# Two gated feed-forward layers behind a chunked attention on one core: operand tiles at fixed places, operand work at four points of a pass, gate-value products behind the sums

## The chip, the cores and the metric

The kernel runs on one core of a Trainium2 chip, as one program. Its metric is device time in microseconds (us): the median of three runs was 1138.36 us (1136.27 to 1138.62). One further execution was taken with the profiler: 1139.58 us, of which 1137.8 us is the span from the first to the last instruction. All rows below come from that one.

## The reference, cut to what matters

```
attention: B=4, H=8, S=768, D=64; chunks of 32 queries, each over 8 memory keys and a window
           (16 to the left, the chunk, 8 to the right); softmax; out -> x [3072 tokens, 512]
moe 1:     gate = 1 / (1 + exp(-(x @ w_gate)))      w_gate, w_val [512, 1536]
           x = (gate * (x @ w_val)) @ w_out         w_out [1536, 512]
moe 2:     h = x @ w_in                             w_in [512, 2048]
           out = (h * (1 / (1 + exp(-h)))) @ w_out  w_out [2048, 512]
```

Weights arrive as 64-bit floats, seen in the kernel as pairs of 32-bit integers.

## The kernel before, in words

Every matrix product is made of three TensorE products of fp32r values: a value is split into a high part (a cast on ScalarE, ACT in the rows) and a low part (value minus high part, on VectorE, DVE). A matmul here is 128x128 by 128x512 unless said otherwise.

A weight tile is loaded as integers (a `stg` tile), scaled on ACT (`rebias`, L126) and joined to fp32 on DVE (`join`, L136 and L139). In this text a *join* is those two DVE instructions.

**Stage 1, blocks 0 to 3.** Tokens go through layer 1 in blocks of 512. For each of 12 slices `f` of the hidden width TensorE (PE) makes `pg` (12 matmuls), `pv` (12), and the output product `y` of the slice before (12 at L104 to L108). ACT makes the sigmoid (L371) and the high part of the gated value (L378); DVE makes gate times value (L376) and the low part (L381). Between these, `steps(0)`, `steps(1)` and `steps(2)` are called after `pg`, after `pv` and after the output product. They carry the attention of the later tiles (`events`: *meet* is scores and the tile before's output, then *exp*, *norm* and *turn*, the transposes to `pt` with the copy to `at`). In block 0 they carry also the layer 1 weights (`Feed.step`), in blocks 1 to 3 the operand work of later stages (`prep.go`). At the end of a block the next block's `x` is split (L96 on ACT, L99 on DVE).

**Stage 2, block -1.** The last 1024 tokens go through layer 1 by a seven-product scheme for 2x2 blocks of the matrices: 12 *passes*, gate (`-1_0g`) and value (`-1_0v`) in turn, then the output product `out2` with 252 matmuls. **Stage 3** takes layer 2 in three blocks (`0_0` to `0_7` are the passes of the first one), each with its `out2` of 336 matmuls.

A pass (`pair2`, L985) makes seven products of six matmuls each, in the order A11, S1, S2, A12, S3, S4, A22, in three PSUM banks: c1 takes A11 and A12, c3 takes S1 and S4, c2 takes S2, S3 and A22. Between two products in one bank the first one has to be read: `s1` (copy of c1, ACT, L1032), `s5` (copy of c3, ACT, L1036, to which GpSimd, POOL, adds s1), the *u sum* (c2 + s1 on DVE, before S3 may start), the *s5 sum* (c2 + s5 on DVE, before A22 may start), then u again from c3 and s1 from c2. Every second pass (odd `p`, not a gate pass) leaves a *tail* to the pass behind it: a difference of two 128x1024 tiles (L973) and the split of one tile for the output product (`gf`, L96 on ACT, L99 on DVE), issued right after the copy `s1`.

**Operand work.** Stages 2 and 3 need the weights in the form of the seven operands, split in high and low. `Pair2` makes them for a pair of layer 2 tiles: two rebias, two joins, four sums of 128x256 (L633), then four tiles `coi` or `coo` (the last one half as long), each with a high cast on ACT (L754) and a low part on DVE (L641), and a store to DRAM. `PairC` does the like for layer 1 (`ccg`, `ccv`, `cco`). `Pace` meters this work: `go(us)` is called at a step of stage 1, or after every second product in a pass (L1012), and runs pieces as long as the given budget lasts; `later` holds a store back for `LAG` calls of `go`, `co` hands out the operand tiles from one pool of 7 buffers (6 in stage 2 and 3) that the loads use too. The pool's next buffer may be written when what used it last is done; for an operand tile that is its store.

Instructions stand on each engine in the order in which the code issues them (`manual_schedule`), so an instruction that waits holds up everything behind it on its engine. All loads and stores go through the queue of SyncE (SP). Weights for a pass come in *granules* (`next_granule`, L954) into five slots.

## Time and profile before

| | |
|---|---|
| median of 3 runs | 1138.36 us |
| profiled execution, own time | 1139.58 us |
| its span | 1137.8 us |
| PE busy | 1097.2 us (96%), 7580 instructions |
| DVE busy | 772.7 us (68%) |
| ACT busy | 534.9 us (47%) |
| POOL busy | 66.7 us (6%) |
| chain of waits that ended last | PE 84%, DMA 8%, DVE 5%, ACT 1%, SP's queue 1% |

PE is busy nearly throughout, so what counts is where it is not, or where it is slow. The busy time of a matmul in the rows has a modelled end, so the distance between the starts of two matmuls is safer than their length. A wait is put down to the engine whose instruction ended last before it; what that instruction itself waited for is read one row further.

### The profile page before, as it was taken

What the parts mean: (1) busy time and instruction counts of PE and PEld (TensorE: products, weight loads), DVE (VectorE), ACT (ScalarE), POOL (GpSimd) and SP (SyncE); (2) the same over time, 40 slices, a digit from 0 to 9 for tenths busy, and PEclk for the clock granted to TensorE, in tenths of its full rate; (3) what the DMA queues carried; (4) which work ended last, traced back from release to release, by engine and by line L of the source; (5) the groups of instructions that cost most, each with busy time, mean ns of one, the idle gap of its engine ahead of it and who ended that gap; (6) DMA issues with size and microseconds to landing.
All of it is one profiled execution on the core that took longest, in us unless ns stands there. A gap on an engine that the chain in (4) does not pass through costs nothing.

```text
span 1137.8 us, 18863 instructions
## 1 busy us (share of the span) xinstructions
PE 1097.2 (96%) x7580; PEld 893.0 (78%) x7580; DVE 772.7 (68%) x1156; ACT 534.9 (47%) x791; POOL 66.7 (6%) x50
## 2 busy tenths in 40 slices
PE   7999999979999999998989997999999999999998
PEld 4888888868777888776777885888888888888887
DVE  7988876667677687566767975458843479543665
ACT  6767554534435453343435544444534455344442
POOL 0000000000000000011110101101011110011000
PEclk9999999989999999999999999999999999999999
DMA  8788678768779897589879586875665666655552
GB/s 330 249 286 296 257 254 298 264 241 286 272 237 319 274 332 282 211 281 323 293 244 384 185 265 240 299 294 186 232 213 194 223 248 226 226 195 204 188 215 78
DMA packets 106247, 288.02 MB, mean 253 GB/s; under 512 B 8624, under 2 KB 39344, under 8 KB 95408
## 3 DMA queue, kind: packets, MB, share of 16 engines
q1 hardware_dynamic: 105872, 286.43, 71.9%
q8 instruction: 60, 0.98, 0.4%
q10 hardware_dynamic: 288, 0.39, 0.1%
q14 instruction: 27, 0.22, 0.1%
HBM read 210.24 MB, written 76.55 MB: 252 GB/s over the span
## 4 chain that ended last, share of the span: by engine, by line
PE 84%; DMA 8%; DVE 5%; ACT 1%; SPq 1%; issue 0%; ACTq 0%; DVEq 0%
PE o L1141 20%; PE c L1005 19%; PE pg L361 11%; PE pv L361 10%; DMA w2o_d<-coo 5%; PE y L104 3%; PE y L106 3%; PE y L108 3%; PE sx L310 1%; PE sx L222 1%; PE o_-1_1_6471 L1141 1%; PE o_-1_0_6470 L1141 1%; PE pt L294 1%; PE c_-1_3g L1005 1%; PE c_-1_1g L1005 1%; PE c_-1_0v L1005 1%
## 5 line engine op out<-in xcount | busy, mean ns | idle before, releaser
L1005 PE MATMUL c<-xp,wr 128*128 128x512 f32 x1008 | 231.7, 391 | 7.1 <-DVE u L970 3.3
L1141 PE MATMUL o<-gf,wr 128*128 128x512 f32 x1008 | 229.0, 389 | 0.0
L1005 PEld LDWEIGHTS c<-xp,wr 128*128 128x128 f32 x1008 | 189.9, 189 | 48.4 <-DVE u L970 3.7
L1141 PEld LDWEIGHTS o<-gf,wr 128*128 128x128 f32 x1008 | 189.2, 188 | 39.3
L361 PE MATMUL pg<-x,w 128*128 128x512 f32 x564 | 138.2, 394 | 6.3 <-ACT x L96 6.2
L361 PE MATMUL pv<-x,w 128*128 128x512 f32 x564 | 139.0, 395 | 2.1 <-DVE sg L376 2.0
L99 DVE TENSOR_TENSOR gf<-g,gf 128x1024 fp32r<-128x1024 f32 x84 | 103.9, 1240 | 50.5 <-ACT gf L96 50.0
L361 PEld LDWEIGHTS pg<-x,w 128*128 128x128 f32 x564 | 106.7, 190 | 29.7 <-ACT x L96 6.7
L96 ACT CAST gf<-g 128x1024 fp32r<-128x1024 f32 x84 | 88.1, 1052 | 86.8 <-PE o L1141 71.4
L361 PEld LDWEIGHTS pv<-x,w 128*128 128x128 f32 x564 | 103.9, 188 | 26.3 <-DVE sg L376 3.0
L970 DVE TENSOR_TENSOR s<-c,s 128x512 f32<-128x512 f32 x48 | 33.2, 691 | 58.4 <-PE c L1005 58.4
L378 ACT CAST g<-sg 128x512 fp32r<-128x512 f32 x48 | 29.7, 620 | 75.3 <-DVE sg L376 75.2
L973 DVE TENSOR_TENSOR g<-g,g 128x1024 f32<-128x1024 f32 x48 | 58.4, 1216 | 0.0
L381 DVE TENSOR_TENSOR g<-sg,g 128x512 fp32r<-128x512 f32 x48 | 33.1, 690 | 35.6 <-ACT g L378 35.6
L976 ACT ACTIVATE g<-s 128x512 f32<-128x512 f32 x48 | 30.3, 632 | 56.2 <-DVE s L970 56.2
L1037 POOL TENSOR_TENSOR s<-s,s 128x512 f32<-128x512 f32 x24 | 35.9, 1497 | 328.9 <-ACT s L1036 280.7
L970 DVE TENSOR_TENSOR u<-c,s 128x512 f32<-128x512 f32 x24 | 16.5, 689 | 49.1 <-PE c L1005 49.1
L371 ACT ACTIVATE sg<-pg 128x512 f32<-128x512 f32 x48 | 28.6, 597 | 28.8 <-PE pg L361 28.6
L271 ACT ACT_TABLE_LOAD x21 | 26.9, 1283 | 30.0 <-DVE e L263 28.1
L104 PE MATMUL y<-g,wor 128*128 128x512 f32 x144 | 40.0, 400 | 0.0
L106 PE MATMUL y<-g,wor 128*128 128x512 f32 x144 | 38.7, 390 | 0.0
L108 PE MATMUL y<-g,wor 128*128 128x512 f32 x144 | 38.6, 390 | 0.0
(596 smaller groups left out, 1565.3 us busy)
## 6 DMA issues: line engine op xcount, KB each, us to landing
wr<-w2o_d SPq DMA_DIRECT2D x42, 1024.0 KB, 4.8
wr<-w2i_d SPq DMA_DIRECT2D x24, 1024.0 KB, 5.3
wor<-wo_d SPq DMA_DIRECT2D x36, 512.0 KB, 6.3
wr<-w2i_d SPq DMA_DIRECT2D x24, 768.0 KB, 4.6
w2o_d<-coo SPq DMA_DIRECT2D x56, 256.0 KB, 6.3
w2i_d<-coi SPq DMA_DIRECT2D x24, 512.0 KB, 7.2
wr<-wc_d SPq DMA_DIRECT2D x12, 1024.0 KB, 6.7
v<-in_vh_dram SPq DMA_DIRECT2D x21, 512.0 KB, 5.5
```

The costliest lines, as they stand in the source:

```text
L96: nc.scalar.copy(hi, src)
L99: lo_eng.tensor_tensor(out=lo, in0=src, in1=hi.bitcast(F32), op=ALU.subtract)
L104: nc.tensor.matmul(o, w_hi, x_hi, start=first, stop=False)
L106: nc.tensor.matmul(o, w_hi, x_lo, start=False, stop=False)
L108: nc.tensor.matmul(o, w_lo, x_hi, start=False, stop=last)
L361: nc.tensor.matmul(o[:, :n], w[:, pw, kt * P : (kt + 1) * P], x[kt][:, px, :n], start=i == 0, stop=i == len(steps) - 1,)
L381: nc.vector.tensor_tensor(out=g[:, 1, :n], in0=sg[:, :n], in1=g[:, 0, :n].bitcast(F32), op=ALU.subtract)
L970: nc.vector.tensor_tensor(out=o, in0=a, in1=b_, op=ALU.add)
L973: nc.vector.tensor_tensor(out=o, in0=a, in1=b_, op=ALU.subtract)
L1005: nc.tensor.matmul(o, w[:, pw, m, kt * P : (kt + 1) * P], X[i][:, px, kt], start=first and j == 0, stop=j == 5, skip_group_check=not first,)
L1037: nc.gpsimd.tensor_tensor(out=s5, in0=s5, in1=s1, op=ALU.add)
L1141: nc.tensor.matmul(c[at[i], dp], w[:, pw, pl, dp * P : (dp + 1) * P], f[:, px, pl], start=i in (A11, S1, S2) and pp == 0 and j == 0, stop= ...
```

## The change

Operand tiles get tags of their own, `co0` to `co3` and, in stage 1, `stg2` and `stg3`, used in turn; loads of `Pair2` go to `stg0` and `stg1`. A tag is taken again only when its store was issued at least three calls of `go` before (`REST`); until then the operand work stands still. Stores are held back for 2 calls instead of 4. In block 0 the loads of layer 1 weights turn over 4 buffers instead of 7; the pool of sigmoid tiles has 4 buffers instead of 5. In a pass `go` is called at four points, with a budget by kind of pass and point, none in the first gate pass. In a value pass the gate-value products (L1026 before, L1057 now) stand behind the DVE sums. In stage 1, for tiles from 8 on, *exp*, *norm* and *turn* come one step later.

```diff
-PREP2 = 0.9
+PREP2 = {"g": (0.4, 0.6, 1.1, 1.1), "v": (0.7, 0.7, 0.3, 0.3), "l": (0.9, 0.9, 1.1, 1.1)}
...
-            self.pool, self.bufs = None, 7
+            self.pool, self.tag = None, None
...
-                [P, 512, 2], I32, tag="stg", name=f"stg_{self.name}", bufs=self.bufs
-            )
+            self.stg = pool.tile([P, 512, 2], I32, tag=self.tag, name=f"stg_{self.name}")
...
-        sg = hold[0].tile([P, 512], F32, tag="sg", name=f"sg{name}", bufs=5)
+        sg = hold[0].tile([P, 512], F32, tag="sg", name=f"sg{name}", bufs=4)
...
+        for n, u in enumerate(units):
+            u.tag = f"stg{n % 4}"
...
-                    events.setdefault(at + 1, []).append(("exp", t))
-                events.setdefault(at + (2 if fast else 4), []).append(("norm", t))
-                events.setdefault(at + (4 if fast else 6), []).append(("turn", t))
+                    events.setdefault(at + 2, []).append(("exp", t))
+                events.setdefault(at + (3 if fast else 4), []).append(("norm", t))
+                events.setdefault(at + (5 if fast else 6), []).append(("turn", t))
...
-                high(0)
-                high(1)
-                yield None
-                for c in range(4):
-                    lo_of(cos[c], f32s[:, 2 * c : 2 * c + cos[c].shape[2]])
-                    pace.later(lambda c=c, co=cos[c]: self.store(c, co))
-                    if c + 2 < 4:
-                        high(c + 2)
-                    yield 0.7 if c < 3 else 0.4
+                for c in range(6):
+                    if c < 4:
+                        while pace.busy():
+                            yield None
+                        high(c)
+                    if c == 1:
+                        yield None
+                    if c >= 2:
+                        c -= 2
+                        lo_of(cos[c], f32s[:, 2 * c : 2 * c + cos[c].shape[2]])
+                        pace.later(lambda c=c, co=cos[c]: self.store(c, co))
+                        yield 0.7 if c < 3 else 0.4
...
-            LAG = 4
+            LAG, REST = 2, 3
...
+            def busy(self):
+                at = self.free[self.tag(self.n)]
+                return at is None or at + self.REST > self.step
...
-                while len(self.fifo) >= self.cap:
-                    self.fifo.pop(0)[1]()
-                return co_tile(pool, name, self.bufs)
+                tag = self.tag(self.n)
+                assert self.free[tag] is not None
+                self.n += 1
+                self.free[tag] = None
+                return co_tile(pool, name, tag)
...
-                if b < 0 or b == 0 and p < NPAIR - 2:
-                    beats[0] += 1
-                    if beats[0] % 2 == 0:
-                        prep.go(PREP2)
...
                 elif kind == "v":
-                    nc.vector.tensor_tensor(out=g, in0=c, in1=g, op=ALU.mult)
+                    wait.append((g, c))
...
+            def mult():
+                while wait:
+                    g, c = wait.pop(0)
+                    nc.vector.tensor_tensor(out=g, in0=c, in1=g, op=ALU.mult)
+
+            def beat(n):
+                if b < 0 or b == 0 and p < NPAIR - 2:
+                    prep.go(PREP2[kind if kind else "l"][n] if p or kind == "v" or b == 0 else 0.0)
...
             prod(c1, A11, True)
             nc.scalar.copy(s1, c1)
             if tail:
                 tail()
+            beat(0)
             prod(c3, S1, True)
             nc.scalar.copy(s5, c3)
             nc.gpsimd.tensor_tensor(out=s5, in0=s5, in1=s1, op=ALU.add)
             if fill:
                 fill()
+            beat(1)
             prod(c2, S2, True)
             add(u2, c2, s1)
             prod(c1, A12, False)
             done("11", c1)
             prod(c2, S3, False)
             add(s5, c2, s5)
+            mult()
             done("22", s5)
+            beat(2)
             prod(c3, S4, False)
             add(u2, c3, u2)
+            mult()
             done("12", u2)
             prod(c2, A22, False)
             add(s1, c2, s1)
             done("21", s1)
+            mult()
+            beat(3)
...
-                prep = Pace(items, 7, 4)
+                prep = Pace(items, ["stg2", "stg3", "co0", "co1", "co2", "co3"])
...
-        prep = Pace([Pair2("o", p, pool) for p in range(NPAIR)], 6, 3)
+        prep = Pace([Pair2("o", p, pool) for p in range(NPAIR)], ["co0", "co1", "co2", "co3"])
```

ACT at the end of block 1, from the sigmoid of the last slice to the split of the next `x`, before:

```order
L371 ACTIVATE sg_11_2913<-pg_11_2900 128x512
L271 ACT_TABLE_LOAD
L271 ACTIVATE e_2950<-e_2950 128x512
L691 CAST cco_0_3006<-fco_2895 128x512
L691 CAST cco_1_3007<-fco_2895 128x512
L96 CAST x_0_3010<-x_2_1835 128x512
```

and now:

```order
L369 ACTIVATE sg_11_2915<-pg_11_2902 128x512
L702 CAST ccv_0_3012<-fcv_2866 128x512
L702 CAST ccv_1_3014<-fcv_2866 128x512
L96 CAST x_0_3016<-x_2_1835 128x512
L96 CAST x_1_3019<-x_2_1835 128x512
L96 CAST x_2_3022<-x_2_1835 128x512
```

The exponential (`e`) is gone from here to the next step, and the two operand casts are of another pair.

DVE from value pass `-1_1v` into gate pass `-1_2g` (`s` stands for the sums called s5 and s1, `u` for the u sum, `g` for gate-value products, the 128x1024 rows are the tail), before, from the s5 sum to the u sum:

```order
L970 TENSOR_TENSOR s_-1_1v<-c_-1_1v,s_-1_1v 128x512
L1026 TENSOR_TENSOR g-1_0_22_5531<-s_-1_1v,g-1_0_22_5531 128x512
L970 TENSOR_TENSOR u_-1_1v<-c_-1_1v,u_-1_1v 128x512
L1026 TENSOR_TENSOR g-1_0_12_5548<-u_-1_1v,g-1_0_12_5548 128x512
L641 TENSOR_TENSOR coo_3_5772<-fo_5657,coo_3_5772 128x256
L970 TENSOR_TENSOR s_-1_1v<-c_-1_1v,s_-1_1v 128x512
L1026 TENSOR_TENSOR g-1_0_21_5559<-s_-1_1v,g-1_0_21_5559 128x512
L973 TENSOR_TENSOR g-1_0_12_5548<-g-1_0_12_5548,g-1_0_11_5522 128x1024
L99 TENSOR_TENSOR gf-1_0_5812<-g-1_0_11_5522,gf-1_0_5812 128x1024
L136 TENSOR_SCALAR stg_w2o_5704<-stg_w2o_5704 128x512
L139 SCALAR_TENSOR_TENSOR fo_5821<-stg_w2o_5704 128x2x256
L970 TENSOR_TENSOR u_-1_2g<-c_-1_2g,s_-1_2g 128x512
```

and now, from the first of two joins (the s5 sum and the product `g..11` stand right ahead of it):

```order
L134 TENSOR_SCALAR stg_w2o_5633<-stg_w2o_5633 128x512
L137 SCALAR_TENSOR_TENSOR fo_5752<-stg_w2o_5633 128x2x256
L998 TENSOR_TENSOR u_-1_1v<-c_-1_1v,u_-1_1v 128x512
L1057 TENSOR_TENSOR g-1_0_22_5524<-s_-1_1v,g-1_0_22_5524 128x512
L998 TENSOR_TENSOR s_-1_1v<-c_-1_1v,s_-1_1v 128x512
L1057 TENSOR_TENSOR g-1_0_12_5533<-u_-1_1v,g-1_0_12_5533 128x512
L1057 TENSOR_TENSOR g-1_0_21_5544<-s_-1_1v,g-1_0_21_5544 128x512
L1001 TENSOR_TENSOR g-1_0_12_5533<-g-1_0_12_5533,g-1_0_11_5515 128x1024
L99 TENSOR_TENSOR gf-1_0_5788<-g-1_0_11_5515,gf-1_0_5788 128x1024
L134 TENSOR_SCALAR stg_w2o_5635<-stg_w2o_5635 128x512
L137 SCALAR_TENSOR_TENSOR fo_5752<-stg_w2o_5635 128x2x256
L998 TENSOR_TENSOR u_-1_2g<-c_-1_2g,s_-1_2g 128x512
```

The low part of an operand (`coo_3`) has left the value pass, one join has come in; the tail and a join still stand ahead of the u sum of the gate pass.

DVE from the tail to the u sum of pass `0_2` in layer 2, before:

```order
L973 TENSOR_TENSOR g_0_12_6948<-g_0_12_6948,g_0_11_6914 128x1024
L99 TENSOR_TENSOR gf_0_7053<-g_0_11_6914,gf_0_7053 128x1024
L136 TENSOR_SCALAR stg_w2o_6943<-stg_w2o_6943 128x512
L139 SCALAR_TENSOR_TENSOR fo_7062<-stg_w2o_6943 128x2x256
L970 TENSOR_TENSOR u_0_2_7044<-c_0_2_7040,s_0_2_7042 128x512
```

and now:

```order
L1001 TENSOR_TENSOR g_0_12_6892<-g_0_12_6892,g_0_11_6865 128x1024
L99 TENSOR_TENSOR gf_0_7009<-g_0_11_6865,gf_0_7009 128x1024
L641 TENSOR_TENSOR coo_0_6991<-fo_6927,coo_0_6991 128x512
L641 TENSOR_TENSOR coo_1_6993<-fo_6927,coo_1_6993 128x512
L641 TENSOR_TENSOR coo_2_7012<-fo_6927,coo_2_7012 128x512
L641 TENSOR_TENSOR coo_3_7015<-fo_6927,coo_3_7015 128x256
L998 TENSOR_TENSOR u_0_2_7000<-c_0_2_6996,s_0_2_6998 128x512
```

Where a join stood, four low parts stand.

## Rows read from the trace of the kernel before

**Rows 1.** Chain that ended last, merged, stages 2 and 3: start us, us, what.
```profile
472.08 2.72 PE c_-1_0g L1005 x12
...
667.13 6.82 PE c L1005 x30
...
753.02 76.16 PE o L1141 x336
```

**Rows 2.** Waits of PE: line waited for, total us, times, longest.
```profile
PE c_-1_2g L1005 <- DVE u_-1_2g L970: 3.4, 1, 3.4
...
PE c_-1_4g L1005 <- DVE u_-1_4g L970: 3.1, 1, 3.1
...
PE pv L361 <- DVE sg L376: 2.0, 3, 1.2
...
PE c_-1_5v L1005 <- DVE s_-1_5v L970: 1.2, 1, 1.2
...
PE o_-1_0_6466 L1141 <- DVE gf-1_2_6460 L99: 1.0, 1, 1.0
...
PE c_-1_0v L1005 <- DVE s_-1_0v L970: 0.5, 1, 0.5
```

**Rows 3.** Timeline of PE: start us, us, instruction, [idle before, releaser].
```profile
248.72 4.67 PE L361 MATMUL pg<-x,w 128*128 128x512 f32 x12 [6.23 <-ACT x L96]
...
483.58 2.25 PE L1005 MATMUL c_-1_0g<-xp-1_6_5433,wr 128*128 128x512 f32 x6 [1.98 <-ACT s_-1_0g L1036]
...
488.15 1.55 PE L1005 MATMUL c_-1_0v<-xp-1_0_5222,wr 128*128 128x512 f32 x6
...
687.15 5.73 PE L1005 MATMUL c<-xp,wr 128*128 128x512 f32 x24 [2.33 <-DVE s L970]
...
699.34 5.96 PE L1005 MATMUL c<-xp,wr 128*128 128x512 f32 x18 [3.27 <-DVE u L970]
```

**Rows 4.** PE by windows of 1 us: us, PE busy (matmuls), granted clock, DMA, GB/s.
```profile
250.00:251.00 1.00, 1.00 (x3) 0.50 1.07 395
...
688.00:689.00 1.00, 1.00 (x6) 1.00 1.01 400
```

**Rows 5.** Timeline of ACT, end of block 1 and pass -1_1v.
```profile
247.53 0.62 ACT L691 CAST cco<-fco 128x512 fp32r<-128x512 f32 x1 [5.21 <-DMA w2i_d<-coi]
...
519.97 0.41 ACT L754 CAST coo<-fo 128x256 fp32r<-128x256 f32 x1 [5.38 <-DMA w2o_d<-coo]
...
521.89 1.05 ACT L96 CAST gf-1_0_5812<-g-1_0_11_5522 128x1024 fp32r<-128x1024 f32 x1
```

**Rows 6.** Timeline of DVE in stage 2, passes -1_0v and -1_2g.
```profile
494.43 1.89 DVE L641 TENSOR_TENSOR coo<-fo,coo 128x512 fp32r<-128x512 f32 x3
...
522.08 1.22 DVE L973 TENSOR_TENSOR g-1_0_12_5548<-g-1_0_12_5548,g-1_0_11_5522 128x1024 f32<-128x1024 f32 x1
523.22 1.22 DVE L99 TENSOR_TENSOR gf-1_0_5812<-g-1_0_11_5522,gf-1_0_5812 128x1024 fp32r<-128x1024 f32 x1
524.35 1.49 DVE L136 TENSOR_SCALAR stg_w2o<-stg_w2o 128x512 int32<-128x512 int32 x1
525.88 0.69 DVE L139 SCALAR_TENSOR_TENSOR fo<-stg_w2o 128x512 int32<-128x512 int32 x1
...
527.08 0.42 DVE L136 TENSOR_SCALAR stg_w2o<-stg_w2o 128x512 int32<-128x512 int32 x1
...
529.60 1.54 DVE L633 TENSOR_TENSOR fo<-fo 128x256 f32<-128x256 f32 x4
```

**Rows 7.** Timeline of POOL, passes -1_1g and -1_2g.
```profile
502.10 1.29 POOL L1037 TENSOR_TENSOR s_-1_1g<-s_-1_1g 128x512 f32<-128x512 f32 x1 [9.03 <-ACT s_-1_1g L1036]
...
523.49 2.07 POOL L1037 TENSOR_TENSOR s_-1_2g<-s_-1_2g 128x512 f32<-128x512 f32 x1 [10.63 <-ACT s_-1_2g L1036]
```

**Rows 8.** Tile coo, its stores: time from issue to landing.
```profile
DMA to landing us min/median/max: 5.2/6.3/8.6
```

**Rows 9.** Line L121, loads into stg tiles: time from issue to landing.
```profile
DMA to landing us min/median/max: 3.4/6.5/10.4
```

More of the change, by code (lines that the diff above doesn't have):

```diff
@@ L532, in pro @@
                     pts[i // 2] = ps_att(f"pt{i}")
-                at = hold[0].tile([P, 512], F32, tag="sg", name=f"at{i}", bufs=5)
+                at = hold[0].tile([P, 512], F32, tag="sg", name=f"at{i}", bufs=4)
                 att_turn(i, pts[i // 2][:, i % 2], at)
@@ L633, in sums_of, with co_tile @@
                 nc.vector.tensor_tensor(out=at[o], in0=at[a], in1=at[b], op=op)
-        def co_tile(pool, name, bufs):
-            co = pool.tile([P, 512, 2], I32, tag="stg", name=name, bufs=bufs)
+        def co_tile(pool, name, tag):
+            co = pool.tile([P, 512, 2], I32, tag=tag, name=name)
             co = co.rearrange("p a b -> p (a b)").rearrange("p (h m k) -> p h m k", h=2, m=2)
@@ L660, in store, with stores @@
                     nc.sync.dma_start(out=out, in_=part)
+            def stores(self, ids, co):
+                if self.k == "o":
+                    for n, i in enumerate(ids):
+                        self.store(i, co[:, :, n])
+                else:
+                    self.store(ids[0], co)
             def whole(self, o, w):
@@ L694, in steps @@
                     lo_of(cos[c], f32s[:, 2 + 2 * c : 4 + 2 * c])
-                    if self.k == "o":
-                        for n, i in enumerate(ids):
-                            pace.later(lambda i=i, co=cos[c][:, :, n]: self.store(i, co))
-                    else:
-                        pace.later(lambda i=ids[0], co=cos[c]: self.store(i, co))
+                    pace.later(lambda ids=ids, co=cos[c]: self.stores(ids, co))
                     yield 0.7
@@ L710, in load @@
             def load(self, pace):
-                for u in self.units:
-                    u.pool, u.bufs = self.pool, pace.bufs
+                for j, u in enumerate(self.units):
+                    u.pool, u.tag = self.pool, f"stg{j}"
                     u.load()
@@ L755, in high, with __init__ @@
                     cos.append(co)
-                high(0)
-                high(1)
-                yield None
-                for c in range(4):
-                    lo_of(cos[c], f32s[:, 2 * c : 2 * c + cos[c].shape[2]])
-                    pace.later(lambda c=c, co=cos[c]: self.store(c, co))
-                    if c + 2 < 4:
-                        high(c + 2)
-                    yield 0.7 if c < 3 else 0.4
+                for c in range(6):
+                    if c < 4:
+                        while pace.busy():
+                            yield None
+                        high(c)
+                    if c == 1:
+                        yield None
+                    if c >= 2:
[3 more added lines that the diff above has]
+                        yield 0.7 if c < 3 else 0.4
         class Pace:
-            LAG = 4
-            def __init__(self, items, bufs, cap):
-                self.due, self.step, self.fifo, self.bufs, self.cap = 0.0, 0, [], bufs, cap
+            LAG, REST = 2, 3
+            def __init__(self, items, tags):
+                self.due, self.step, self.fifo, self.tags = 0.0, 0, [], tags
+                self.free, self.n = {t: -9 for t in tags}, 0
                 self.items, self.urgent, self.gen = list(items), [], None
@@ L777, in __init__, with tag, put @@
                 twos[0].load(self)
-            def co(self, pool, name):
-                while len(self.fifo) >= self.cap:
-                    self.fifo.pop(0)[1]()
-                return co_tile(pool, name, self.bufs)
+            def tag(self, n):
+                return self.tags[n % len(self.tags)]
+            def busy(self):
+                at = self.free[self.tag(self.n)]
+                return at is None or at + self.REST > self.step
+            def co(self, pool, name):
+                tag = self.tag(self.n)
[3 more added lines that the diff above has]
+                return co_tile(pool, name, tag)
             def later(self, store):
                 self.fifo.append((self.step, store))
+            def put(self):
+                self.fifo.pop(0)[1]()
+                tag = next(self.tag(n) for n in range(self.n, self.n + 9) if self.free[self.tag(n)] is None)
+                self.free[tag] = self.step
             def advance(self):
@@ L801, in go @@
                 while self.fifo and self.fifo[0][0] <= self.step - self.LAG:
-                    self.fifo.pop(0)[1]()
+                    self.put()
                 self.due = min(self.due + us, 2.5)
@@ L816, in finish @@
                 while self.advance() is not False:
-                    pass
+                    if self.busy():
+                        self.step += self.REST
+                        while self.fifo:
+                            self.put()
                 while self.fifo:
-                    self.fifo.pop(0)[1]()
+                    self.put()
         g_t, wo_u, yacc = {}, {}, {}
@@ L831, in sg_slot @@
         def sg_slot(name):
-            return hold[0].tile([P, 512], F32, tag="sg", name=name, bufs=5)
+            return hold[0].tile([P, 512], F32, tag="sg", name=name, bufs=4)
         def emit_out1(bi, f, tile_of=sg_slot):
@@ L1062, in pair2 @@
             return tail_of
-        gf, beats = {}, [0]
+        gf = {}
         def npp_of(b):
```

8 lines of the change are left out of this document (5 added, 3 removed).

## The prediction

> **What bounds the kernel now.** I read the chain of waits first. In stages 2 and 3 it is matmuls almost alone, so the time is the number of matmuls times their duration plus what PE loses between them. A 128x512 matmul takes 76.16 / 336 = 0.2267 us [rows 1]; a product of six 1.36, a pass of 42 9.52. The starts of the stages in the chain then give the losses. Stage 2 lasts 667.13 - 472.08 = 195.05 us for 12 passes, the output product of stage 1's last slice (12 matmuls) and 252 of `out2`, 768 in all, or 174.1: 20.95 lost. The first eight passes of stage 3 last 753.02 - 667.13 = 85.89 for 76.17: 9.7 lost. The `out2` that follows from 753.02 on is at full speed, and behind it I look for nothing [rows 1].
>
> The waits of PE name what the losses are: the u sum of the gate passes `-1_2g` and `-1_4g` (3.4 and 3.1), the s5 sum of the six value passes (0.5 the first, 1.2 the last), three waits for the gated value in stage 1 (2.0 together) and 1.0 at the start of `out2` [rows 2]. The timeline of PE adds the largest, 6.23 before 12 matmuls at the end of block 1, 1.98 in `-1_0g`, and in stage 3 2.33 and 3.27 [rows 3].
>
> A gap costs more than its length when the clock falls. The 12 matmuls behind the 6.23 took 4.67 and not 2.72; the 18 behind the 3.27 took 5.96 and not 4.08: 1.95 and 1.9 more. The 24 behind 2.33 took 5.73, 0.29 above 5.44; the 12 behind 1.98, up to the next pass at 488.15, took 4.57 and not 2.72 [rows 3]. The granted clock was 0.50 (1.2 GHz) in the first of these stretches and 1.00 (2.4 GHz) in the one behind 2.33 [rows 4]. So gaps of 3.3 and 6.2 were followed by a slow stretch, one of 2.33 was not, and one of 1.98 was: from about 2 to 3 it is open.
>
> Then what the waited-for engines themselves wait for. ACT's operand cast `cco` stood 5.21 for a store of another operand tile, with the split of the next `x` queued behind it; `coo` stood 5.38 in `-1_1v`, with the `gf` cast behind it [rows 5]. These are DMA landings (5.2 to 8.6 us after issue [rows 8]) that reach PE by way of an ACT queue. On DVE three low parts (1.89 for three) stand ahead of the s5 sum in the first value pass, and the tail (two of 1.22) and a join (1.49 and 0.69) ahead of the u sum of `-1_2g` [rows 6].
>
> **The change, part by part.**
>
> *Fixed places with REST.* An operand tile's high cast now comes at least three calls of `go` after its store was issued. In stages 2 and 3 a call comes every quarter of a pass (2.4 us) and in stage 1 every output step; together with the held store and the turn of the tags I count four to five steps, 11 us or more, from store to reuse, against landings up to 8.6 [rows 8]. So ACT's waits for stores should go. In stage 1 the 6.23 of idle falls to about 0.6 (the split itself and its way to PE), with the 1.95 of slow clock: 7.6. The three waits for the gated value (2.0) come from ACT held up in the same way, and go. Against it, block 0: a load now waits for the join four units back instead of seven, so some have 5.5 to 7 us to land, while landing takes 3.4 to 10.4, median 6.5 [rows 9]. PE and DVE have slack in block 0; I put it at 0.5 (bounds 0 and the rival below). Four sigmoid buffers can hold a sigmoid up by a store of y, at a block's start, behind work that covers it: nothing, and if that cover is gone up to the three waits' 2.0. Stage 1: **9.1**.
>
> *`-1_0g`.* There is no operand work in it now, so no rebias in front of its s5 copy. Its 1.98 of wait and the 1.85 behind it (4.57 - 2.72) go: **3.8**.
>
> *Value passes.* The lows ahead of the s5 sum and the gate-value products are gone; products come behind sums. The s5 sum can start when its product ends, as DVE has no other work then. The residue of stage 2's 20.95, after 3.8 for `-1_0g`, 5.3 for `-1_2g` and 5.0 for `-1_4g` (waits of 3.4 and 3.1 [rows 2] with 1.9 of clock each) and 1.0 for `out2`, is 5.8: the six waits of 0.5 to 1.2, with a restart behind each. Gain **5.8**. If I am wrong, and the join put into the value pass lies before a sum, 0.3 a pass come back.
>
> *`-1_2g`.* Here is what stays. Count from the pass's start, when A22 of the pass before ends. S3 may start at 5.44 (four products), if the u sum has read c2. DVE, spaced as in [rows 6] (0.6 for a 512-wide operation, 1.14 for a 1024-wide one): the s5 sum begins at -2.72, and behind it product, join, u sum, product, s1 sum and two products end at 2.8; the tail at 5.05. The second join's first part costs 0.42 alone, but 1.49 beside POOL's add [rows 6]; that add took 2.07 then and 1.29 elsewhere [rows 7]. In this pass it should run from about 3.9, so the join's first part ends at 5.95, its second at 6.6 and the u sum at 7.3: a gap of 1.9. Without the meeting of the two the u sum would end at 6.8, 0.5 earlier.
>
> *`-1_4g`.* By the same walk, with two lows and the tail ahead of the u sum and no join: 1.4.
>
> *`out2`.* The last sums no longer have products ahead of them, so its first `gf` is ready: 1.0 gained.
>
> Stage 2 would lose 1.9 + 1.4 = 3.3 before any clock price, where it lost 20.95: **17.65**.
>
> *Stage 3, first block.* `0_1`: two rebias on ACT, two joins and four sums (1.54 [rows 6]) ahead of the u sum: 1.0. `0_2`: ACT casts two operand tiles ahead of the s1 copy, so the `gf` cast (1.05 [rows 5]) ends late; then DVE's half of it, four lows (about 2.2 by 1.89 for three [rows 6]) and the u sum, ending at 8.0: 2.6. `0_4`: tail and two joins, the second beside POOL's add: 8.2, so 2.8 (1.9 without it). Together 6.4 where 9.7 were lost: **3.3**. Bounds: nothing is lost (9.7), or the walks are 1 us worse in each (0.3).
>
> *The clock.* Three gaps of 1.9 to 2.8 remain (`-1_2g`, `0_2`, `0_4`), in the open region. If all are followed by a slow stretch they cost 3 x 1.95 = 5.9, if none 0. The nearest rows stand on both sides (2.0 yes, 2.33 no), so I take half, 2.9, and 0.5 for restarts: **-3.4**.
>
> Beside POOL: both operations that met its add in the rows grew, 1.49 for 0.42 and 2.07 for 1.29 [rows 6, 7], while the 1024-wide sum with two inputs in SBUF that ran into the same add kept its 1.22 [rows 6]. The Trainium skill, GPSIMD Engine Reference, section 1 "Specifications", says that GpSimd shares its SBUF interfaces with VectorE and contends with instructions in a 2-port mode or with two SBUF inputs. For the join the trace agrees; for the two-input sum, read by its own length, it does not. By the rule, the sums and lows that I moved next to POOL's add (in `0_1` and `0_2`) would make that add, and the s5 sum behind it, later still; by the rows only the joins do, which the walks of `-1_2g` and `0_4` hold.
>
> **Sum.** 9.1 + 17.65 + 3.3 - 3.4 = 26.65. The profiled execution of 1139.58 would be 1112.9. It lies 1.22 above the median of the runs, 1138.36, so the median becomes 1111.7: **1112**.
>
> **Rivals.**
>
> *A, the stalls that I leave go too.* DVE in `-1_2g` and `0_4` is ahead of my walk, the joins miss POOL's add (0.5 and 0.9 less) and no gap brings the slow clock (2.9 less). For: a 2.33 gap left the clock at 1.00 [rows 3, 4]; the walks chain spacings that were read where DVE was loaded. Against: tail and join together are fixed work of 4 us and more. All gaps halved (3.3 + 6.4 to 4.9) and no clock price: 26.65 + 4.8 + 2.9 = 34, or about 1104.
>
> *B, the DMA waits move and don't go.* A store held back two calls still lies in SP's queue behind loads, and six tiles per pair in six buffers came round to the same place before too; what REST counts is calls, and in stage 1 calls that come close together leave less time than landings of 8.6 [rows 8]. Then operand casts still wait on ACT, with the x split and `gf` behind them. For: the 5.21 and 5.38 are of this kind [rows 5]. Against: the distances counted above. Half of stage 1's gain (4.5) and stage 3's (3.3) go, and all three gaps bring the slow clock (3.0): 1112 + 10.8, about 1123. If the tail passes moreover keep their old losses (10.3 instead of 3.3), 1130.
>
> *C, slower.* Block 0 becomes bound by loads. With four buffers each load is issued only when the join four units back is done; if the queue of SP takes each to the upper landing, 10.4, where a unit's turn leaves 7 [rows 9], a slice of block 0 waits about 3 us, and over 11 slices that is 33, more than the 26.65 gained. It decides above 26.65 / 11 = 2.4 a slice. Then 1138 + 6, about 1145. For: loads of 6.5 in the median leave little. Against: only some loads are that short of time, and the weights for a slice are wanted later than their joins.
>
> *D, nothing changes:* that would need the same loss on PE at other places; the order shows the work gone from the two largest, so little chance.
>
> **How the numbers follow.** My case 0.58, A 0.14, B 0.20, C 0.05, D 0.03. What this kernel's measurement can tell from no change is about 0.2%, 2.3 us. The likeliest case alone spans 1106 (no price for the clock, 2.9; nothing for block 0, 0.5; walks half a us too long at five places, 2.5) to 1119 (all three clock drops, 3.0; walks 1 us too short at four places). Range with most of A and B: 1102 to 1125. Faster: my case, A and nearly all of B, 0.92; same 0.03; slower 0.05.
>
> **What to look for afterwards.** Right, if ACT shows no operand cast that waited for a store for some us; if the gap at the end of block 1 is under 1 us; if value passes take 9.5 and `-1_0g` 12.2; and if PE's waits are now at `-1_2g`, `-1_4g`, `0_1`, `0_2` and `0_4`, on the u sum. Wrong, if one of these gaps is above 3; if ACT's `DMA` waits in block 1 or pass `0_2` still reach 3 us; or if block 0 ends later than before by more than a few us, with loads as what DVE or ACT waited for.

## The result, and the profile after

The changed kernel takes 1123.47 us (median of four runs, 1122.33 to 1124.43) against 1138.49 for the kernel before: a ratio of 0.9871 (95% interval 0.9853 to 0.9888). The profiled execution took 1124.10, 15.5 less than that of before, with a span of 1122.1. So it is faster, by 1.3%, and inside the range, but 15 us were gained where 27 were forecast.

What PE waits for after the change, longest in total first (total us, times, longest):

```profile
PE c L1033 <- DVE u L998: 8.4, 3, 3.5
PE sx L308 <- ACT at L293: 2.5, 2, 2.3
PE c_-1_2g L1033 <- DVE u_-1_2g L998: 2.5, 1, 2.5
PE c_-1_4g L1033 <- DVE u_-1_4g L998: 2.4, 1, 2.4
...
PE c_-1_4v L1033 <- DVE u_-1_4v L998: 0.9, 1, 0.9
PE c_-1_0v L1033 <- DVE u_-1_0v L998: 0.8, 1, 0.8
```

Against [rows 2]: the waits for s5 sums are gone, the wait for the gated value too, and what is left is on u sums; three of these, 8.4 together, are in stage 3 (the first line). The timeline of PE, at the end of block 1, early in block 3, and in stage 3:

```profile
241.66 2.88 PE L359 MATMUL pg<-x,w 128*128 128x512 f32 x12
...
367.73 0.86 PE L308 MATMUL sx<-v,at 64*32 64x64 f32 x64 [2.33 <-ACT at L293]
...
662.98 11.41 PE L1033 MATMUL c<-xp,wr 128*128 128x512 f32 x42 [2.03 <-DVE u L998]
677.93 22.14 PE L1033 MATMUL c<-xp,wr 128*128 128x512 f32 x84 [3.54 <-DVE u L998]
702.85 34.59 PE L1033 MATMUL c<-xp,wr 128*128 128x512 f32 x144 [2.79 <-DVE u L998]
```

The first line answers to the 6.23 of [rows 3]: no gap, and 12 matmuls in 2.88. The last three are in passes `0_1`, `0_2` and `0_4`. Before, `0_1` had the gap of 2.33 and `0_2` that of 3.27 and one of 1.52 on the s1 copy. So the gaps of `0_1` and `0_2` are shorter now, by 0.3 and 1.25, and the one in `0_4` is new. But now the matmuls are slow behind each of the three (11.41 for 42, which take 9.52 at full speed), where before they were behind the 3.27 alone. The clock, behind the gap of `-1_4g` and behind that of `0_1` (us, PE busy, granted clock, DMA, GB/s):

```profile
555.00:556.00 1.00, 1.00 (x6) 1.00 0.98 296
...
664.00:665.00 1.00, 1.00 (x4) 0.50 1.09 384
```

On ACT, operand casts no longer stand five microseconds for a store, as two did in [rows 5]; in the whole trace these are the casts with a DMA named as what ended their wait:

```profile
239.25 1.14 ACT L702 CAST ccv<-fcv 128x512 fp32r<-128x512 f32 x2 [3.90 <-DMA wor<-wo_d]
689.67 0.62 ACT L761 CAST coo<-fo 128x512 fp32r<-128x512 f32 x1 [0.56 <-DMA w2o_d<-coo]
694.07 0.41 ACT L761 CAST coo<-fo 128x256 fp32r<-128x256 f32 x1 [0.20 <-DMA w2o_d<-coo]
```

The first is put down to a load of `wor`, and an earlier one, at 165.14, to a load of `q`. In run e1 below the first one's wait is as long and is put down to the DVE sums that make its input; in both traces the cast begins 1.1 us after these sums do, so it is they that it waits for, and no DMA. PE loses nothing behind either.

```profile
239.26 1.14 ACT L702 CAST ccv<-fcv 128x512 fp32r<-128x512 f32 x2 [3.89 <-DVE fcv L633]
```

The stores of `coo` land no faster than in [rows 8], and the loads only 0.9 faster in the median than in [rows 9]:

```profile
DMA to landing us min/median/max: 4.8/6.9/8.2
```

```profile
DMA to landing us min/median/max: 3.5/5.6/9.3
```

And DVE with POOL, in `-1_2g`, `0_2` and `0_4`, where [rows 6, 7] stood:

```profile
507.86 1.59 POOL L1072 TENSOR_TENSOR s_-1_2g<-s_-1_2g 128x512 f32<-128x512 f32 x1 [8.30 <-ACT s_-1_2g L1071]
508.23 2.31 DVE L99 TENSOR_TENSOR gf-1_0_5788<-g-1_0_11_5515,gf-1_0_5788 128x1024 fp32r<-128x1024 f32 x1
...
510.46 0.42 DVE L134 TENSOR_SCALAR stg_w2o<-stg_w2o 128x512 int32<-128x512 int32 x1
510.91 0.69 DVE L137 SCALAR_TENSOR_TENSOR fo<-stg_w2o 128x512 int32<-128x512 int32 x1
511.52 0.68 DVE L998 TENSOR_TENSOR u_-1_2g<-c_-1_2g,s_-1_2g 128x512 f32<-128x512 f32 x1
...
673.97 3.30 DVE L641 TENSOR_TENSOR coo<-fo,coo 128x512 fp32r<-128x512 f32 x4
674.19 1.60 POOL L1072 TENSOR_TENSOR s<-s,s 128x512 f32<-128x512 f32 x1 [13.28 <-ACT s L1071]
...
699.24 1.28 POOL L1072 TENSOR_TENSOR s<-s,s 128x512 f32<-128x512 f32 x1 [9.21 <-ACT s L1071]
699.25 1.81 DVE L137 SCALAR_TENSOR_TENSOR fo<-stg_w2o 128x512 int32<-128x512 int32 x1
```

Here lies the first surprise: a low part, join or operand sum on DVE that begins while POOL adds grows by some 1.1 us, a `gf` half from 1.22 to 2.31, four lows from 2.2 to 3.30, a join's second part from 0.69 to 1.81. The u sum is queued behind it. The u sum itself, which reads a PSUM bank, does not grow: in ten passes it begins inside the add, and keeps its length, as in `-1_1g`:

```profile
488.62 1.29 POOL L1072 TENSOR_TENSOR s_-1_1g<-s_-1_1g 128x512 f32<-128x512 f32 x1 [9.02 <-DVE fo L633]
489.37 0.69 DVE L998 TENSOR_TENSOR u_-1_1g<-c_-1_1g,s_-1_1g 128x512 f32<-128x512 f32 x1 [0.78 <-PE c_-1_1g L1033]
```

Where each run lost time, worked out from the starts of the passes on PE (a pass's length less 9.52, that of `-1_0g` less 12.24, that of the eight passes of stage 3's first block less 76.16). The columns of losses are from the one profiled execution of each run, the last one is the median of all of its executions; the two differ most in e4 (profiled 1126.73) and e5 (1124.70). In stage 1 the changed kernel, e3 to e8, e11 and e12 are alike, and yet `-1_0g` starts anywhere from 462.1 to 464.1 in them, so differences of up to 2 us in that column say nothing. (More than half of it is the gap of 2.3 in block 3: the matmuls behind it are slow in e3, e4, e6 and e7 and not in the others.)

| run | start of -1_0g | -1_0g | six value passes | -1_2g | -1_4g | stage 3, first block | median us |
|---|---|---|---|---|---|---|---|
| before | 471.9 | 4.0 | 5.4 | 5.3 | 5.0 | 9.7 | 1138.5 |
| changed | 462.2 | 0 | 2.3 | 4.4 | 2.7 | 15.3 | 1123.5 |
| e1 no rest | 462.1 | 0 | 2.3 | 4.4 | 1.6 | 16.6 | 1123.9 |
| e2 old events | 461.8 | 0 | 2.3 | 4.2 | 2.7 | 14.8 | 1122.3 |
| e3 old points | 463.1 | 3.2 | 0 | 2.0 | 2.1 | 4.6 | 1112.0 |
| e4 products inline | 464.1 | 0 | 2.3 | 4.1 | 4.1 | 15.2 | 1122.8 |
| e5 add on DVE | 462.1 | 1.3 | 3.8 | 2.2 | 2.1 | 13.3 | 1126.8 |
| e6 late add | 464.0 | 0 | 0.1 | 1.7 | 1.6 | 8.0 | 1115.6 |
| e7 quiet tails | 463.9 | 0 | 8.8 | 0 | 0 | 4.7 | 1114.9 |
| e8 quiet, late | 462.1 | 0 | 4.0 | 0 | 0 | 3.7 | 1110.9 |
| e9 no rest, late stores | 463.9 | 0 | 2.3 | 4.4 | 1.6 | 29.5 | 1139.0 |
| e10 before, early stores | 466.4 | 3.9 | 4.6 | 2.0 | 2.0 | 3.6 | 1120.4 |
| e11 quiet best | 462.1 | 0 | 0 | 0 | 0 | 0 | 1099.7 |
| e12 places alone | 462.3 | 3.0 | 4.6 | 2.0 | 2.0 | 6.1 | 1116.5 |

### The profile page after: what moved, and what is told of

It is laid out like the page before. It is cut to its first block, busy times and chain, and to the rows that moved or that the text cites. A ratio compares the mean times of both kernels' runs of the same rounds, so it can differ in the third digit from the quotient of the medians.

```text
span 1122.1 us, 18930 instructions
## 1 busy us (share of the span) xinstructions
PE 1093.2 (97%) x7580; PEld 893.7 (80%) x7580; DVE 776.6 (69%) x1156; ACT 533.1 (48%) x791; POOL 65.6 (6%) x50
## 5 line engine op out<-in xcount | busy, mean ns | idle before, releaser
L1033 PE MATMUL c<-xp,wr 128*128 128x512 f32 x1008 | 235.9, 397 | 8.4 <-DVE u L998 8.4
L1033 PEld LDWEIGHTS c<-xp,wr 128*128 128x128 f32 x1008 | 193.2, 192 | 50.6 <-DVE u L998 9.6
L359 PEld LDWEIGHTS pg<-x,w 128*128 128x128 f32 x564 | 104.4, 188 | 22.1 <-DVE x L99 0.7
L317 DVE STREAM_TRANSPOSE x<-sx 128x512 f32<-128x512 f32 x20 | 14.3, 716 | 33.8 <-PE sx L220 30.3
```

The lines of the kernel that those rows point to most:

```text
L359: nc.tensor.matmul(o[:, :n], w[:, pw, kt * P : (kt + 1) * P], x[kt][:, px, :n], start=i == 0, stop=i == len(steps) - 1,)
L1033: nc.tensor.matmul(o, w[:, pw, m, kt * P : (kt + 1) * P], X[i][:, px, kt], start=first and j == 0, stop=j == 5, skip_group_check=not first,)
```

## The experiments

Two questions: which part of the change made the gain, and what ate the 11 us that are missing. My theory for the first was the fixed places with their rest; for the second, DVE's queue ahead of the u sums together with POOL's add. All runs but e10 start from the changed kernel.

**Without the rest (e1).**

```diff
-            LAG, REST = 2, 3
+            LAG, REST = 2, 0
```

> The changed kernel with REST 0: a fixed place may be taken again as soon as its store has been issued, so the operand cast waits on ACT for the store to land (5 to 9 us). Theory: the rest of three calls is what took the 6.2 us gap at the end of block 1 and the waits in stage 3 away; 6 to 12 us come back, 1129 to 1136, and ACT shows casts that wait for w2i_d or w2o_d by 3 us or more. Rival (the gain of stage 1 is that of the later exponentials, and the places hardly matter): within 2 us of 1123.5.

1123.88: the theory fell. On ACT a cast waits for a store by 1.6 us at the most. A place that is free once its store has been issued does as well as one that rests for three calls.

**Late stores as well (e9).**

```diff
-            LAG, REST = 2, 3
+            LAG, REST = 4, 0
```

> The changed kernel with REST 0 and stores held back for 4 calls as before. Theory (since REST itself proved to do nothing: the stores issued two calls earlier are what freed the places in time): operand casts wait on ACT for stores again, by 3 us or more in block 1 and in stages 2 and 3; 4 to 10 us slower, 1127 to 1134. Rival (places of their own, apart from the loads, did it): 1122 to 1126, no cast waits over 2 us.

1138.98, worse than either: the whole gain is gone, but not as I had put it. Block 1 and stage 1 are as in the changed kernel (463.9, within the spread given above), and no cast waits for a store there, so there the places of their own are enough to keep casts from waiting (the operand work still stands until a place's store has been issued); the later events are in e9 too. All is lost in stage 3 (29.5), where the cast waits for stores again, with the s1 copy and the `gf` cast behind it. ACT in pass `0_2`:

```profile
673.10 0.62 ACT L761 CAST coo<-fo 128x512 fp32r<-128x512 f32 x1 [2.18 <-DMA w2o_d<-coo]
674.89 0.62 ACT L761 CAST coo<-fo 128x512 fp32r<-128x512 f32 x1 [1.17 <-DMA w2o_d<-coo]
675.41 0.58 ACT L1066 COPY s<-c 128x512 f32<-128x512 f32 x1
675.89 1.05 ACT L96 CAST gf<-g 128x1024 fp32r<-128x1024 f32 x1
...
680.19 0.40 ACT L761 CAST coo<-fo 128x256 fp32r<-128x256 f32 x1 [2.73 <-DMA w2o_d<-coo]
```

Late stores under a rest of three calls were not tried.

**Early stores alone (e10).** The kernel before, with one number changed:

```diff
-            LAG = 4
+            LAG = 2
```

> The kernel before with stores held back for 2 calls instead of 4, nothing else. Theory (early stores): the 5.21 and 5.38 waits on ACT go, with the 6.23 gap on PE; 8 to 15 us faster than before, 1123 to 1130. Rival (shared places): 1136 to 1140, the waits stay.

1120.39: this number alone gains 18 us, where the whole change gains 15. The waits for stores in stages 2 and 3 fall to 0.9 at most, and in `-1_1v` the 5.38 of [rows 5] is gone. In block 1 the theory was too wide: the wait stays, 4.49 instead of 5.21, and with it a gap:

```profile
245.32 0.62 ACT L691 CAST cco<-fco 128x512 fp32r<-128x512 f32 x1 [4.49 <-DMA w2i_d<-coi]
```

```profile
246.51 4.37 PE L361 MATMUL pg<-x,w 128*128 128x512 f32 x12 [4.11 <-ACT x L96]
```

So of stage 1's 9.7 us early stores alone give 5.5, and the places with late stores (e9) 8, each good to some 2 us.

**Old events (e2).**

```diff
-                    events.setdefault(at + 2, []).append(("exp", t))
-                events.setdefault(at + (3 if fast else 4), []).append(("norm", t))
-                events.setdefault(at + (5 if fast else 6), []).append(("turn", t))
+                    events.setdefault(at + 1, []).append(("exp", t))
+                events.setdefault(at + (2 if fast else 4), []).append(("norm", t))
+                events.setdefault(at + (4 if fast else 6), []).append(("turn", t))
```

> The changed kernel with exp, norm and turn of the later tiles at the steps of before. Theory: at most 2 us slower (1122 to 1126), as the gap at the end of block 1 came from a cast that waited for a store. Rival (the exponential and its table load ahead of the x split made the gap): some 6 to 9 us come back, 1130 to 1133.

1122.30, as the theory had it: the later events are worth nothing here. They give the x split 0.86 us and cost PE the 2.33 of block 3, a gap that e2 does not have. With them the copy of `at` that PE waits for stands on ACT behind the cast of the gated value; ACT in the changed kernel:

```profile
365.60 0.62 ACT L376 CAST g<-sg 128x512 fp32r<-128x512 f32 x1 [2.77 <-DVE sg L374]
...
367.08 0.60 ACT L293 COPY at<-pt 128x512 f32<-128x512 f32 x1
372.98 0.60 ACT L369 ACTIVATE sg<-pg 128x512 f32<-128x512 f32 x1 [5.30 <-DMA yd<-y]
```

The last row is a sigmoid that stands for a store of `y`, as four buffers allow; PE has no gap behind it, and one of 0.3 at most in e2, where the same wait is 6.21. And e2 beside e10 shows what the places do: both have early stores and the old events, and the gap at the end of block 1 is 0.86 with places and 4.11 without.

**Old points (e3).** `go(0.9)` after every second product, as before, in place of the four budgets:

```diff
                 if i in final:
                     next_granule()
+                if b < 0 or b == 0 and p < NPAIR - 2:
+                    beats[0] += 1
+                    if beats[0] % 2 == 0:
+                        prep.go(0.9)
...
             def beat(n):
-                if b < 0 or b == 0 and p < NPAIR - 2:
-                    prep.go(PREP2[kind if kind else "l"][n] if p or kind == "v" or b == 0 else 0.0)
+                pass
```

> The changed kernel with the operand work called as before, 0.9 us after every second product, the first gate pass too. Theory: the points and budgets made the gain in stage 2; the gap of 2 us in -1_0g with its slow clock comes back (3.8), and lows stand ahead of the s5 sum in value passes again (0.5 to 1.2 each); stage 3 may gain. 1125 to 1133. Rival (fixed places alone make the whole gain): 1121.5 to 1125.

1112.03, 11.4 us faster than the changed kernel, and outside both expectations: the four points with their budgets are what cost the time. (The two were not taken apart here, but e7 below keeps the points, changes the budgets, and gets 8.6 of the 11.4.) With the old ones three lows of an operand lie between the u sum and the s5 sum of a value pass, where DVE is free, and in tail passes one join stands ahead of the u sum beside the tail, where with the new ones there are up to four lows or two joins. Only `-1_0g` is worse (3.2), as foreseen. DVE in `-1_0v` of e3:

```profile
482.81 0.69 DVE L998 TENSOR_TENSOR u_-1_0v<-c_-1_0v,s_-1_0v 128x512 f32<-128x512 f32 x1 [3.23 <-PE c_-1_0v L1033]
483.42 1.89 DVE L641 TENSOR_TENSOR coo<-fo,coo 128x512 fp32r<-128x512 f32 x3
485.53 0.69 DVE L998 TENSOR_TENSOR s_-1_0v<-c_-1_0v,s_-1_0v 128x512 f32<-128x512 f32 x1 [0.23 <-issue]
```

**Products inline (e4), and places alone (e12).** In e4 the products go back to where they stood; in e12 the old points come with them, so that DVE's order in the passes is that of before.

```diff
-                    wait.append((g, c))
+                    nc.vector.tensor_tensor(out=g, in0=c, in1=g, op=ALU.mult)
```

> The changed kernel with the gate-value products where they stood before, each right behind its sum's copy, the first one ahead of the s5 sum. Theory: that product can start at 5.5 us into the pass and is done before the s5 sum's product ends at 6.8, so nothing changes: 1122 to 1125. Rival (the order of the products is what took the 0.5 to 1.2 us waits of the value passes away): 0.76 in each of six passes, 1127 to 1129.

> The changed kernel with the operand work called as before after every second product and the gate-value products inline as before; left of the change are the fixed places, the stores two calls earlier, the turn-over in block 0 and the later events. Theory: DVE's order in the passes is that of before, so the value passes lose 0.76 each again and the tail passes one product more: 5 to 9 us slower than with old points alone (1112.0), 1117 to 1121, and still 17 to 21 faster than before by the waits for stores that are gone. Rival (the order of the products is worth nothing, as under the four points): 1111 to 1114.

e4: 1122.82, no change that its spread (1119.4 to 1126.7) would let one see. e12: 1116.48, 4.5 slower than e3: with old points the order of the products does count, 0.76 in each value pass. DVE in `-1_0v` of e12 shows how: the product waits for its bank, the lows queue behind it, and the s5 sum behind them.

```profile
481.95 0.69 DVE L998 TENSOR_TENSOR u_-1_0v<-c_-1_0v,s_-1_0v 128x512 f32<-128x512 f32 x1 [3.24 <-PE c_-1_0v L1033]
483.26 0.69 DVE L1054 TENSOR_TENSOR g-1_0_11_5522<-c_-1_0v,g-1_0_11_5522 128x512 f32<-128x512 f32 x1 [0.61 <-PE c_-1_0v L1033]
483.87 1.89 DVE L641 TENSOR_TENSOR coo<-fo,coo 128x512 fp32r<-128x512 f32 x3
485.67 0.68 DVE L998 TENSOR_TENSOR s_-1_0v<-c_-1_0v,s_-1_0v 128x512 f32<-128x512 f32 x1
```

Two parts of the change thus do the same job, and only one of them is needed: either the products go behind the sums or the lows leave that place.

**POOL's add, moved in two ways (e5, e6).** In e5 it is DVE's, in e6 it stands behind the u sum, held there by an addition on eight elements that reads it (a result nothing uses):

```diff
-            nc.gpsimd.tensor_tensor(out=s5, in0=s5, in1=s1, op=ALU.add)
+            nc.vector.tensor_tensor(out=s5, in0=s5, in1=s1, op=ALU.add)
```

```diff
-            nc.gpsimd.tensor_tensor(out=s5, in0=s5, in1=s1, op=ALU.add)
...
             add(u2, c2, s1)
+            mark = p2.tile([P, 8], F32, tag="mark", name=f"mark_{n}", bufs=2)
+            nc.gpsimd.tensor_tensor(out=mark, in0=u2[:, :8], in1=u2[:, :8], op=ALU.add)
+            nc.gpsimd.tensor_tensor(out=s5, in0=s5, in1=s1, op=ALU.add)
```

> The changed kernel with the addition of s1 to s5 (passes and, of pair2 only) on DVE instead of POOL, at the same place in the program. Theory (POOL's add makes the DVE instruction beside it wait for about 1.1 us, and that delays the u sums): DVE gets 0.6 more work in each pass, but no low part, join or sum is lengthened (gf 1.22 and not 2.31 in -1_2g, lows 2.2 and not 3.3 in 0_2); the gaps shrink by about 0.5 each, 2 to 5 us faster with what the clock gives back: 1118.5 to 1121.5. Rival (the gaps are the queue of work alone, POOL costs nothing): 0.6 more at each of seven gaps, 1126 to 1130.

> The changed kernel with POOL's add put behind the u sum in every pass of pair2 (a tiny POOL instruction that reads the u sum holds it there). Theory: the u sums of -1_2g, -1_4g, 0_1, 0_2, 0_4, -1_0v and -1_4v come about 1.1 earlier, so gaps of 2.5, 2.4, 2.0, 3.5, 2.8, 0.8 and 0.9 become 1.4, 1.3, 0.9, 2.4, 1.7, 0 and 0 (7.3 less) and most of the slow stretches (9 us) go: 1109 to 1116. Rival (queue of work alone): no change, 1122 to 1125.

e6: 1115.61, 7.9 faster, inside the theory's range. Every gap shrank by what was forecast for it: 2.45 to 1.36, 2.40 to 1.31, 2.03 to 1.06, 3.54 to 2.48, 2.79 to 1.68, 0.75 and 0.90 to nothing. DVE in `-1_2g` of e6, to be laid beside the same rows of the changed kernel:

```profile
508.98 1.22 DVE L99 TENSOR_TENSOR gf-1_0_5796<-g-1_0_11_5517,gf-1_0_5796 128x1024 fp32r<-128x1024 f32 x1
510.12 0.42 DVE L134 TENSOR_SCALAR stg_w2o<-stg_w2o 128x512 int32<-128x512 int32 x1
510.57 0.69 DVE L137 SCALAR_TENSOR_TENSOR fo<-stg_w2o 128x512 int32<-128x512 int32 x1
511.18 0.68 DVE L998 TENSOR_TENSOR u_-1_2g<-c_-1_2g,s_-1_2g 128x512 f32<-128x512 f32 x1
512.01 0.20 POOL L1078 TENSOR_TENSOR mark_-1_2g<-u_-1_2g 128x8 f32<-128x8 f32 x1 [9.94 <-DVE u_-1_2g L998]
512.17 1.29 POOL L1079 TENSOR_TENSOR s_-1_2g<-s_-1_2g 128x512 f32<-128x512 f32 x1
```

e5: 1126.78, slower by 3.3, against the theory's number, although most gaps at the old places did shrink by 0.5 (2.45 to 1.90, 2.40 to 1.84, 2.03 to 1.48, 3.54 to 3.07, 0.90 to 0.41; not that of `0_4`, 2.82). What I had left out: DVE runs in order, and the add waits there for ACT's copy of c3, 3.34 us of idle time in `-1_0g`, 2.90 in `-1_0v` and 0.4 to 1.3 in others, with joins queued behind it. So passes which lost nothing now wait for their u sum (0.97 in `-1_0g`, 0.77 in `-1_2v`, 0.57 in `-1_3g`), `-1_0v` waits 1.67 instead of 0.75, and the last two blocks of stage 3, which are in no column of the table and lose nothing in the changed kernel, lose 1.0 each. The profiled execution, the fastest of the four, is only 0.6 slower than that of the changed kernel; where the median loses the rest is not shown.

```profile
479.38 0.69 DVE L1072 TENSOR_TENSOR s_-1_0v<-s_-1_0v 128x512 f32<-128x512 f32 x1 [2.90 <-ACT s_-1_0v L1071]
```

**Quiet tails (e7), with the late add (e8).** Other budgets, and a call of `go` with a budget of nothing does no work. The condition on `tail` also held for passes that have no tail, so no gate pass, and in layer 2 only the first pass, had work at its first two points:

```diff
+                if us == 0:
+                    return
...
-                    prep.go(PREP2[kind if kind else "l"][n] if p or kind == "v" or b == 0 else 0.0)
+                    if kind == "g":
+                        us = (0.0, 0.0) if tail or not p else (0.6, 0.6)
+                        us += (0.0, 1.2) if not p else (1.2, 1.2)
+                    elif kind == "v":
+                        us = (1.2, 1.2, 0.0, 0.0) if p % 2 else (1.2, 1.2, 0.6, 0.6)
+                    else:
+                        us = (0.0, 0.0, 1.2, 1.2) if tail else (1.2, 1.2, 1.0, 1.0)
+                        us = (1.2, 1.2, 1.2, 1.2) if not p else us
+                    prep.go(us[n])
```

> The changed kernel with other budgets: no operand work at the first two points of passes that begin with a tail nor at the last two of the pass before in stage 2, more at the others; POOL's add as it is. Theory: the u sum of the tail passes has only the tail ahead of it; gaps of about 1 us are left in -1_2g and -1_4g (products, tail and POOL's add), none or under 1 in stage 3: 15 less of 24 lost: 1106 to 1113. Rival (ACT's casts or transfers set the gaps): over 1118.

> The budgets of the run with quiet tails and POOL's add behind the u sum. Theory: no gap over 0.5 us in stage 2 and 3, no slow clock: 24 us lost there become 2: 1099 to 1106. Rival: POOL's late add delays the s5 sum, new gaps there; no faster than the quiet tails alone.

1114.86 and 1110.86: both short of the theory. The tail passes of stage 2 lost nothing, as expected; but the work that left them was put ahead of the u sums of the value passes, which now wait 1.1 to 1.6 us (0.4 to 0.6 with the late add). That no tail is near does not make a place cheap.

**The version that puts it together (e11).** The old points, none in `-1_0g`; in a pass with a tail the call between u and s5 sum comes behind the s5 sum, and POOL's add behind the u sum, there only:

```diff
+                if us == 0:
+                    return
...
+            quiet = p and p % 2 == 0 and kind != 'v'
...
+                if b < 0 or b == 0 and p < NPAIR - 2:
+                    beats[0] += 1
+                    if beats[0] % 2 == 0 and not (quiet and i == A12):
+                        prep.go(0.0 if kind == 'g' and not p else 0.9)
...
             def beat(n):
-                if b < 0 or b == 0 and p < NPAIR - 2:
-                    prep.go(PREP2[kind if kind else "l"][n] if p or kind == "v" or b == 0 else 0.0)
+                pass
...
-            nc.gpsimd.tensor_tensor(out=s5, in0=s5, in1=s1, op=ALU.add)
+            if not quiet:
+                nc.gpsimd.tensor_tensor(out=s5, in0=s5, in1=s1, op=ALU.add)
...
             add(u2, c2, s1)
+            if quiet:
+                mark = p2.tile([P, 8], F32, tag="mark", name=f"mark_{n}", bufs=2)
+                nc.gpsimd.tensor_tensor(out=mark, in0=u2[:, :8], in1=u2[:, :8], op=ALU.add)
+                nc.gpsimd.tensor_tensor(out=s5, in0=s5, in1=s1, op=ALU.add)
...
             add(s5, c2, s5)
             mult()
+            if quiet and (b < 0 or b == 0 and p < NPAIR - 2):
+                prep.go(0.9)
```

> The changed kernel with the operand work called as before after every second product (none in the first gate pass), but in passes with a tail the call between the u sum and the s5 sum put behind the s5 sum, and POOL's add put behind the u sum in these passes only. Theory: no pass has operand work ahead of a u sum that is late, and the add meets nothing: gaps under 0.4 in all passes, no slow clock in stages 2 and 3; what is left without a loss there is a span of 1097, so 1099 to 1102. Rival (DVE's tail and products alone make gaps of 1 us or more): 1105 to 1110.

1099.66 us, 0.9658 of before (interval 0.9642 to 0.9674); the span is 1097.1, where 1097 had been worked out, and the mean granted clock of the span 1.00. The longest waits of PE are now these; none is in stage 2 or 3:

```profile
PE sx L308 <- ACT at L293: 2.5, 2, 2.3
PE warm L490 <- POOL ident masks.py:199: 1.4, 1, 1.4
PE pg L346 <- ACT x L561: 1.3, 2, 0.9
```

## Why the prediction was right in its sign, and too large by 11 us

Stage 1: 9.1 forecast, 9.7 measured, good to some 2 us. The path was the one named, a store's landing that reached PE through ACT's queue, but not the means: I credited the rest, and e1 shows that it does nothing. Places of their own (e9) and early stores (e10) each act without it. The sigmoid buffers, priced at nothing, cost nothing; the later events, for which the sum has no term, took 2.33 in block 3.

`-1_0g`: 3.8 forecast, 4.0 measured. `out2`: 1.0 and 1.2. Value passes: 5.8 forecast, 3.1 measured; the s5 sums are on time in all six, as said, but in `-1_0v` and `-1_4v` the u sum came late (0.75 and 0.90), by a join or four sums that had met POOL's add.

The step that failed first is "by the rows only the joins do" in the part on POOL. I had read a `gf` half that kept its 1.22 beside the add [rows 6, 7] as an instruction that does not mind it. In truth that instruction had begun first, and the add had waited for it: 2.07 instead of 1.29. The Trainium skill, GPSIMD Engine Reference, section 1 "Specifications", names DVE instructions with two inputs in SBUF; the trace after agrees, with 2.31 for 1.22 and with the u sum, which has only one input there and keeps its 0.69, and so does e6 with 7.9 us. The rule that I weighed and set aside was the right one, only that DVE and not just the add pays: in these traces who begins second waits. So the walks were short by 0.6 in `-1_2g` (1.9 forecast, 2.45; the walk let the meeting cost 0.5, and it cost 1.1), 1.0 in `-1_4g` (1.4, 2.40), 1.0 in `0_1` (1.0, 2.03) and 0.9 in `0_2` (2.6, 3.54), right in `0_4` (2.8, 2.79), where the collision had been in the walk. With the two value passes this is 5.2 us.

The second step that failed is the price of the clock, for which the sum took half. Five gaps above 2 us instead of three, and four of them were followed by a slow stretch: 42 matmuls in 11.41 (1.9 too many), 84 in 22.14 (3.1), 144 in 34.59 (1.95), and 1.9 in `-1_2g`. With the restarts some 9.7 were lost where 3.4 stood in the sum, 6.3 more. Together 11.5; with 0.6 that stage 1 gave beyond its term, and tenths either way in the other terms, that is the missing 11.

Stage 3, for which a gain of 3.3 had been credited, lost 5.6 more than before, by both. Here the old points would have gained 5.2 (e3); I compared the new order with the old trace, and never the new points with the old ones under the new places, which was the comparison that mattered.

Of the signs named beforehand most came true: the gap at the end of block 1 and the casts' waits for stores are gone or under 0.6, `-1_0g` takes its 12.2, and PE waits in the five passes named. But two value passes take 10.6 and 10.7, not 9.5, and one sign of being wrong came true as well, a gap above 3 (3.54 in `0_2`).

Of the rivals, the time is that of B (1123), but its mechanism is not what happened: no cast waited on a store by more than 0.6. That the time still lies in the range, 1.5 us from its end, is luck: the forecast's own case ended at 1119, and the range goes further on account of B. C did not come about: block 0 is no later than before. A needed what only e11 has.

## What to carry to other kernels

A change in several parts has to be priced part by part against the others: here a stores' delay of two calls instead of four was worth 18 us by itself, the places some 4 more (e12 against e10), and the new points with their budgets cost 11 of it. Where an engine runs in order, look for the spot in each period in which it is idle by its data (here between the u sum and the s5 sum) and put extra work there, not ahead of the sum that TensorE waits for. And when two instructions overlap in a trace, ask which began first before saying that one does not disturb the other.

## What the runs showed of the hardware

Unexpected was how sharp the exchange between POOL and DVE is: in the changed kernel a 128x512 add of 1.29 on POOL puts 0.98 to 1.12 on the low part, join or operand sum on DVE that begins inside it, in seven passes, and moving it gave back 0.97 to 1.11 at each of five gaps. The u sum, with one input in a PSUM bank, begins inside the add in ten passes, 0.27 to 0.77 after its start, and keeps its 0.69.

What a gap does to the clock is not told by its length alone. In the trace of before a gap of 1.98 in `-1_0g` was followed by a slow stretch, in e12 the same gap of 1.98 was not; 2.03 and 2.45 were in the changed kernel, 2.40 was not, nor was 2.90 in e10 (228 matmuls behind it in 52.24, granted clock 1.00). Even the same gap at the same place goes either way. That of 2.03 in `0_1` was followed by a slow stretch in the changed kernel, and the like ones in e2 and e4 were not. And in stage 1, where e6 runs the same code as the changed kernel, the gap in block 3 is 2.33 in one and 2.28 in the other; 2.3 and 1.6 us behind its end, in the changed kernel first and then in e6 (us, PE busy, granted clock, DMA, GB/s):

```profile
370.00:371.00 1.00, 1.00 (x6) 1.00 0.98 313
...
370.00:371.00 1.00, 1.00 (x34) 0.50 0.96 270
```

Of the gaps of 1.3 to 1.9 looked at in the tail passes (e1, e3, e5, e6, e10, e12), none was. What told 2.40 from 2.45 stays open.
